# Coarse and fine factor tables of an S4D kernel stored the other way round, with a new order of the work

## The chip, the cores and the metric

The kernel runs on one core of one Trainium2 chip. The metric is the time of one execution on the device in microseconds (us); lower is better. The core's engines work side by side, each through its own list of instructions: TensorE (PE in the profile, with PEld for its weight loads), VectorE (DVE), ScalarE (ACT), GpSimd (POOL) and SyncE (SP), which issues most DMAs here. They wait for each other through semaphores.

## What is computed

The reference is one layer of two blocks on a sequence of 2048 positions with 512 channels, in float32. The first is a diagonal state-space convolution, done with Fourier transforms; the second is a gated MLP:

```python
P = exp((A * dt[:, None])[:, :, None] * pos)         # 512 channels x 128 states x 2048 positions
K = 2.0 * einsum("dn,dnl->dl", C, P).real            # the convolution's kernel
y = irfft(rfft(u, 2L) * rfft(K, 2L))[:L] + u * D_skip
h = x + y(layernorm(x))
z = gelu(layernorm(h) @ w_in)                        # two halves z1, z2
g = w_sp @ layernorm(z2) + b_sp                      # w_sp is 2048 x 2048
out = h + (z1 * g) @ w_out
```

The change touches only the first block, where `P` and `K` are made, and the passage to the second. `A` has a negative real part (the rate of decay) and an imaginary part (the turning).

## The kernel before

**The first block** (`phase_a`) works on the channels in four chunks of 128. For each chunk it makes `K` in eight units of 16 channels (`unit`), and takes `K` and the normed input through transforms that are matrix products: `piece_c` and `piece_d` for `K`, `piece_a` and `piece_b` for the input, the product of the two spectra in `piece_d` (the VectorE multiplication in place in `trio`), and `piece_e` back into `big`. Each kind has eight pieces to a chunk. The spectrum of the input is needed with its two partition halves also swapped; `exchange` makes this copy with two DMAs of 1 MB, `b[:64] <- a[64:]` and `b[64:] <- a[:64]`.

In a unit, sine and cosine come from ScalarE, and the decay from GpSimd. A position is split in two: exp(-rate * position) is a coarse factor times a fine factor. `table` makes all 34 factors for 64 channels (three GpSimd multiplications of rates with the constants `c_lt`, one ScalarE Exp, and one GpSimd multiplication of the last factors with the states' weights). It keeps them in a tile `mt` of [34 factors, 64 channels]: factor by factor, so that two factors of one channel lie 64 numbers apart. A unit then makes three products of 16 channels x 32 positions (8 coarse x 4 fine factors) into `m_bufs`, which lie in the tile `wa`:

```python
ta = mt[:, a0:a0 + 4, d0:d0 + 16].rearrange("p s d -> p d s").unsqueeze(2).to_broadcast([P, 16, 8, 4])
tb = mt[:, b0:b0 + 8, d0:d0 + 16].rearrange("p s d -> p d s").unsqueeze(3).to_broadcast([P, 16, 8, 4])
nc.gpsimd.tensor_tensor(m[:, i, :].rearrange("p (d b a) -> p d b a", d=16, a=4), tb, ta, op=ALU.mult)
```

**The order of the first block** is written out. Every operation is first recorded in a `Plan`. Three tables of characters then say at which place each operation is issued (`RANKS`), on which of two engines it runs where there is a choice (`FORMS`: a copy out of PSUM on ScalarE or VectorE; part of the layernorm's scaling on ScalarE or GpSimd; some small subtractions and products on VectorE or GpSimd) and which PSUM bank it takes (`BANKS`). All of them are issued from `Plan.issue`, which is why nearly every row of this block names line L251.

**The end of the first block.** The last chunk's spectra are multiplied in two parts, channels 0 to 23 and 24 to 31 of each group of 32 (`split`), so that six of the eight pieces back can run before the last units are done. Operations after the last one that touches a generator's buffer (`cut`) are issued by `rest`. Beside them the first weight `w1` of the second block is split into a rounded and a remaining half (`w1h`, `w1l`): four quarters, each a ScalarE copy and a VectorE subtraction, in the buffers `wa` and `wb`. They are issued after the last spectrum product and after the copy out of the piece back numbered 6. The second block starts with `lines` (matmuls into `y`), which read all of `big`.

**The second block** (`phase_b1` to `phase_b3`) is the larger part of the span. Its code and order are left as they are.

## Time and profile before

| | us |
|---|---|
| median of 3 runs | 869.35 (867.56 to 872.04) |
| the profiled execution, its own time | 870.07 |
| span of its instructions | 868.3 |
| first matmul of `lines` (second block) | 321.16 |
| PE busy, share of the span | 808.4, 93% |
| DVE, ACT, POOL busy | 658.1, 467.2, 326.9 |

The profile gives for each engine how long it was busy, in which groups of instructions, and after which wait each one started. "Releaser" is what ended a wait. "issue" stands for time in which the engine waited for nothing that the profile shows. PEclk is the clock that TensorE was granted, 1.00 being the full one. Times in the timeline count from the start of the span. A matmul of float32 numbers stands as two instructions in the timeline (a piece back has 8 products and 16 instructions). DMA queue q1 carries what SyncE issues; q8 carries instructions to the engines, 16 KB in a packet.

### The profile page before, as it was taken

Reading aid. Unit: us, or ns where it says so; the run is one execution under the profiler, and the core shown is the slowest. Engines: PE = TensorE matmul, PEld = TensorE weight load, DVE = VectorE, ACT = ScalarE, POOL = GpSimd, SP = SyncE. Lnnn points to the kernel's source line nnn. Section 1 sums busy time; section 2 is a strip of 40 time slices with the busy share of each in tenths; the row PEclk is TensorE's granted clock in tenths of the full one; section 3 lists DMA queues with packets and bytes.
Section 4 is the critical chain, followed back from the end, with each engine's and each line's share of the span. In section 5 each row is a group of like instructions: output and inputs, shape, how many; then the busy total and the mean of one; then the engine's idle time right before and its main releaser. Section 6 shows DMA issues by size and latency. Waiting matters only on the chain.

```text
span 868.3 us, 17467 instructions
## 1 busy us (share of the span) xinstructions
PE 808.4 (93%) x6813; PEld 694.9 (80%) x6813; DVE 658.1 (76%) x1254; ACT 467.2 (54%) x782; POOL 326.9 (38%) x338
## 2 busy tenths in 40 slices
PE   1379989999898989999999999999999999999998
PEld 0267879889796989888899988888888888887886
DVE  6889999999797539776056778989875985777733
ACT  6679879999897323436223245557434533344211
POOL 6879879999887100000015210123312002223200
PEclk9989999999999979999999999999999999999999
DMA  9212422401307556735216314799979547799832
GB/s 340 76 76 64 100 64 66 108 24 27 84 2 205 205 211 195 182 85 200 92 50 151 80 50 130 178 205 233 239 174 231 187 133 181 158 198 239 207 102 80
DMA packets 63874, 121.81 MB, mean 140 GB/s; under 512 B 6736, under 2 KB 21200, under 8 KB 61488
## 3 DMA queue, kind: packets, MB, share of 16 engines
q1 hardware_dynamic: 52160, 99.33, 37.6%
q0 software_dynamic: 11632, 21.37, 15.1%
q8 instruction: 53, 0.87, 0.4%
q14 instruction: 29, 0.24, 0.1%
HBM read 92.89 MB, written 19.40 MB: 129 GB/s over the span
## 4 chain that ended last, share of the span: by engine, by line
PE 59%; DMA 2%; DVE 1%; issue 0%; ACT 0%; SPq 0%; DVEq 0%; ACTq 0%; POOLq 0%
PE m L1139 28%; PE pz L834 9%; PE pz L934 9%; PE po L1062 7%; PE y L747 4%; PE pl L1062 2%; DMA raws<-in_w_sp_dram 1%; DMA zo<-scr_z 1%; DVE c L1154 0%; DVE c L1092 0%; DVE gz L672 0%; PE lnh_pv L778 0%; DVE wts L672 0%; PE lnh_pm L764 0%; DVE zc_wb L672 0%
## 5 line engine op out<-in xcount | busy, mean ns | idle before, releaser
L1139 PE MATMUL m<-wts,zc_wa 128*128 128x512 f32 x700 | 217.5, 390 | 0.0
L1139 PEld LDWEIGHTS m<-wts,zc_wa 128*128 128x128 f32 x700 | 131.4, 188 | 28.0
L251 POOL TENSOR_TENSOR wa<-mt 128x512 f32<-128x512 f32 x96 | 148.1, 1565 | 12.4 <-PE ps L251 4.6
L1010 POOL DMA_DIRECT2D raws<-in_w_sp_dram x64 | 58.1, 996 | 210.3 <-DMA raws<-in_w_sp_dram 207.7
L1139 PE MATMUL m<-wts,zc_wb 128*128 128x512 f32 x350 | 136.5, 390 | 0.0
L671 ACT CAST wts<-raws 128x512 fp32r<-128x512 f32 x112 | 69.0, 619 | 55.3 <-DMA raws<-in_w_sp_dram 27.2
L672 DVE TENSOR_TENSOR wts<-raws,wts 128x512 fp32r<-128x512 f32 x112 | 76.4, 684 | 16.4 <-ACT wts L671 16.3
L934 PE MATMUL pz<-w,ht 128*128 128x448 f32 x384 | 77.4, 363 | 0.0
L1139 PEld LDWEIGHTS m<-wts,zc_wb 128*128 128x128 f32 x350 | 65.7, 188 | 14.1
L940 POOL TENSOR_SCALAR sm<-sm 128x1 f32<-128x1 f32 x16 | 5.5, 343 | 188.7 <-DVE sm L939 188.7
L934 PEld LDWEIGHTS pz<-w,ht 128*128 128x128 f32 x384 | 72.0, 187 | 5.3
L834 PE MATMUL pz<-ht,w1h 128*128 128x512 f32 x224 | 71.2, 395 | 0.0
L251 ACT ACTIVATE ps<-wb 128x512 f32<-128x512 f32 (+1 forms) x80 | 65.6, 826 | 9.6 <-DVE trio L251 4.1
L251 PE MATMUL ps<-c_inv,trio 128*128 128x128 f32 x512 | 63.4, 282 | 1.3 <-DVE trio L251 1.3
L1062 PE MATMUL po<-w,gz 128*128 128x512 f32 x252 | 62.8, 396 | 1.4 <-DVE gz L672 1.4
L251 PEld LDWEIGHTS ps<-c_inv,trio 128*128 128x128 f32 x512 | 60.6, 196 | 4.3 <-DVE trio L251 1.9
L251 PE MATMUL ps<-big,a 128*128 128x128 f32 (+2 forms) x512 | 63.4, 283 | 0.5 <-ACT big L251 0.2
L251 PEld LDWEIGHTS ps<-big,a 128*128 128x128 f32 x512 | 60.5, 196 | 3.2 <-ACT big L251 0.9
L671 ACT CAST zc_wa<-raws 128x384 fp32r<-128x384 f32 (+1 forms) x70 | 37.1, 533 | 40.9 <-DVE raws L1044 26.1
L1062 PEld LDWEIGHTS po<-w,gz 128*128 128x128 f32 x252 | 47.2, 188 | 13.2 <-DVE gz L672 1.8
L251 ACT COPY big<-ps 128x512 f32<-128x512 f32 x56 | 32.1, 581 | 34.9 <-PE ps L251 34.6
L251 DVE TENSOR_TENSOR trio<-ps,trio 128x1024 f32<-128x1024 f32 (+2 forms) x36 | 38.1, 1104 | 15.8 <-PE ps L251 15.8
(163 smaller groups left out, 1570.3 us busy)
## 6 DMA issues: line engine op xcount, KB each, us to landing
raws<-in_w_sp_dram SPq DMA_DIRECT2D x112, 256.0 KB, 4.1
raws<-in_w_sp_dram POOLq DMA_DIRECT2D x80, 256.0 KB, 5.7
trio<-trio SPq DMA_DIRECT2D x8, 1024.0 KB, 9.5
g<-in_c_g_dram SPq DMA_DIRECT2D x8, 1024.0 KB, 6.3
scr_z<-zo SPq DMA_DIRECT2D x28, 256.0 KB, 2.3
big<-in_u_a_dram SPq DMA_DIRECT2D x8, 512.0 KB, 6.8
xq<-in_u_b_dram SPq DMA_DIRECT2D x4, 1024.0 KB, 6.7
scr_h<-xq SPq DMA_DIRECT2D x16, 256.0 KB, 5.1
```

What stands on the lines that cost most here:

```text
L251: r = getattr(getattr(self.nc, e), method)(*map(self.real, args), **{k: self.real(x) for k, x in kw.items()})
L671: nc.scalar.copy(hi, src)
L672: nc.vector.tensor_sub(lo, src, hi.bitcast(F32))
L747: nc.tensor.matmul(ys[n, g][:, i, :], gt[:, i, r, :], qv[:, r, l0 + i], start=(r == 0), stop=(r == 1))
L834: nc.tensor.matmul(pt, w[:, q, f], ht[n][k][:, q], start=(q == 0 and i == 0), stop=(q == 3 and i == 2))
L934: nc.tensor.matmul(pt[:, :FQ], a[:, q], w2[:, b, q, f], start=(q == 0 and i == 0), stop=(q == 3 and i == 2))
L940: nc.gpsimd.tensor_scalar_add(sm[:, 14:15], sm[:, 13:14], 1e-5)
L1010: nc.gpsimd.dma_start(r, ws[1], accum_op=ALU.add)
L1062: nc.tensor.matmul(pt, gz[fb][x][:, P * a:P * a + P], wo[:, y, fb, w], start=(first and fb == fbs[0] and i == 0), stop=(last and fb == fbs ...
L1139: nc.tensor.matmul(pt, x[:, f], y, start=(k == 0 and i == 0), stop=(k == KT - 1 and i == 2))
```

## The change

- `mt` becomes [64 channels, 34 factors]: the factors of one channel lie next to each other. There are now 4 coarse and 8 fine factors to 32 positions, where there were 8 and 4. The products are written in runs of eight fine factors, and the number of factors stays 34. The multiplications that make the table have the same number of elements (748 + 714 + 714 = 2176, as 768 + 704 + 704 before); the one with the weights has 256 where it had 512.
- `exchange` gets an order between its two DMAs: the second now waits until the first has landed (`two["after"] = one`, "half by half").
- The last chunk's spectra are multiplied in two parts of 16 and 16.
- The quarters of `w1` are split one by one, each right after a copy out of one of the last chunk's last four pieces back.
- `RANKS`, `FORMS` and `BANKS` are new throughout. Three scalings of the layernorm go from GpSimd to ScalarE, three subtractions from GpSimd to VectorE, three copies from ScalarE to VectorE and two small ones too. ScalarE's table loads go from 15 to 18 ahead of the second block.

Three places of the new order, each with the names as the order lists them.

**ScalarE at the end of the first block**, before and after. `big<-ps` is the copy out of a piece back, `w1h<-w1r` the rounding of quarters of `w1`, x4 four of them in a row. Before:

```order
L251 COPY big<-ps_103 128x128x4
L251 COPY big<-ps_101 128x128x4
L251 COPY big<-ps_100 128x128x4
L251 COPY big<-ps_102 128x128x4
L671 CAST w1h<-w1r 128x896 x4
L251 COPY big<-ps_100 128x128x4
```

Now:

```order
L250 COPY big<-ps_101 128x128x4
L250 COPY big<-ps_100 128x128x4
L675 CAST w1h<-w1r 128x896 x2
L250 COPY big<-ps_102 128x128x4
L675 CAST w1h<-w1r 128x896
L250 COPY big<-ps_100 128x128x4
L675 CAST w1h<-w1r 128x896
```

Four roundings stood ahead of the last copy out of a piece back. Now one stands directly ahead of it, and one behind.

**SyncE at the second of the four exchanges**, before and after, with the semaphores that each DMA waits for. `trio<-trio` is half an exchange, `sw` a unit's matmul weights, `wa<-scr_xhat` the normed input of a later piece. Before:

```order
L251 DMA trio<-trio 64x4096 [waits DMAHW7_49,DVE_49,PE_49]
L251 DMA trio<-trio 64x4096 [waits DMAHW0_49]
L251 DMA wa<-scr_xhat 128x256 [waits DMAHW1_49,PE_49]
L251 DMA sw_91<-scr_stk 96x512 [waits DMAHW5_49,DMAHW2_49,PE_49]
L251 DMA wa<-scr_xhat 128x256 [waits DMAHW3_49,PE_49]
```

Now:

```order
L250 DMA trio<-trio 64x4096 [waits DMAHW7_49,DVE_49,PE_49]
L250 DMA trio<-trio 64x4096 [waits DMAHW7_49,DMAHW0_49]
L250 DMA sw_91<-scr_stk 96x512 [waits PE_49]
L250 DMA wa<-scr_xhat 128x256 [waits DMAHW2_49,PE_49]
L250 DMA wa<-scr_xhat 128x256 [waits DMAHW3_49,PE_49]
```

The second half has the first half's semaphore (DMAHW7) among those it waits for, and the loads behind it on SyncE wait with it.

**TensorE behind the last unit**, whose last product is the row `wa,wb`. `ks` is the first transform of `K` (`piece_c`), `big,a` the second (`piece_d`), `c_inv` the way back (`piece_e`), `y` the second block. Before:

```order
L251 MATMUL ps_102<-wa,wb 32x64 x16
L251 MATMUL ps_100<-c_inv,trio 128x128 x8
L251 MATMUL ps_101<-c_inv,trio 128x128 x5
L251 MATMUL ps_103<-wb,ks_81 64x128 x8
L251 MATMUL ps_101<-c_inv,trio 128x128 x3
L251 MATMUL ps_100<-c_inv,trio 128x128 x8
L251 MATMUL ps_102<-big,a_78 128x4x8 x16
L251 MATMUL ps_103<-big,a_78 128x4x8 x16
L251 MATMUL ps_101<-c_inv,trio 128x128 x8
L251 MATMUL ps_102<-c_inv,trio 128x128 x8
L251 MATMUL ps_100<-c_inv,trio 128x128 x8
```

Now, up to the fourth of eight pieces back (four more `c_inv` rows of x8 follow, and then `y`):

```order
L250 MATMUL ps_100<-wa,wb 32x64 x16
L250 MATMUL ps_102<-wb,ks_80 64x128 x8
L250 MATMUL ps_100<-wb,ks_81 64x128 x8
L250 MATMUL ps_101<-c_inv,trio 128x128 x8
L250 MATMUL ps_103<-c_inv,trio 128x128 x8
L250 MATMUL ps_102<-big,a_78 128x4x16 x8
L250 MATMUL ps_100<-big,a_78 128x4x16 x8
L250 MATMUL ps_101<-c_inv,trio 128x128 x8
L250 MATMUL ps_103<-big,a_78 128x4x16 x8
L250 MATMUL ps_102<-big,a_78 128x4x16 x8
L250 MATMUL ps_100<-c_inv,trio 128x128 x8
```

Behind the last product stood 48 products of pieces back; now there are 64, and one more `ks` row. The 32 of `big,a` stay.

The diff, with the tables cut to a line each:

```diff
 RANKS = (
-    "06000407010V090G0M050P0A0J080D0d0Z0g03020B0E0F0H0I0K0L0N0O0T0W0Y0a0c0R0e0f0i0j0l0q0s0v0z0+1011121415181T1I1X221e2326292D"
+    "05000608010709040B0F0A0R0M0V0I0f0Z0j03020C0E0G0H0J0K0L0O0Q0S0U0X0Y0a0N0b0d0m0g0l0o0r0u0z10121316181A1D1Y1O1a1d1h1t221w25"
...
     lt = np.concatenate([
-        28 - 4 * np.arange(8), 1 + np.arange(3), 3 - np.arange(4), 64 * (1 + np.arange(3)),
-        32 + 4 * np.arange(8), 256 * np.arange(8),
+        24 - 8 * np.arange(4), 1 + np.arange(7), 7 - np.arange(8), 64 * (1 + np.arange(7)),
+        32 + 8 * np.arange(4), 512 * np.arange(4),
     ]).astype(f8)
...
     def issue(self, o):
...
+        if "after" in o:
+            info = mybir.DependencyInfo(mybir.DependencyClass.Sync, mybir.DependencyReason.DATA)
+            self.tc.add_manual_dep(r.ins, o["after"]["ins"].name, info, reason="half by half")
+        o["ins"] = r.ins
         return r
...
-    mts = [one(g1, f"mt{h}", [34, 64]) for h in range(2)]
+    mts = [one(g1, f"mt{h}", [64, 34]) for h in range(2)]
...
-        for lo, n in ((0, 12), (12, 11), (23, 11)):
-            nc.gpsimd.tensor_tensor(mt[:, lo:lo + n], rc[:, 64 * h:64 * h + 64].unsqueeze(1).to_broadcast([P, n, 64]),
-                                    c_lt[:, lo:lo + n].unsqueeze(2).to_broadcast([P, n, 64]), op=ALU.mult)
+        for lo, n in ((0, 22), (22, 21), (43, 21)):
+            nc.gpsimd.tensor_tensor(mt[:, lo:lo + n], rc[:, 64 * h + lo:64 * h + lo + n].unsqueeze(2).to_broadcast([P, n, 34]),
+                                    c_lt.unsqueeze(1).to_broadcast([P, n, 34]), op=ALU.mult)
         nc.scalar.activation(mt, mt, AF.Exp)
-        nc.gpsimd.tensor_tensor(mt[:, 26:34, :], mt[:, 26:34, :],
-                                rc[:, P + 64 * h:P + 64 * h + 64].unsqueeze(1).to_broadcast([P, 8, 64]), op=ALU.mult)
+        nc.gpsimd.tensor_tensor(mt[:, :, 30:], mt[:, :, 30:],
+                                rc[:, P + 64 * h:P + 64 * h + 64].unsqueeze(2).to_broadcast([P, 64, 4]), op=ALU.mult)
...
-        for i, (a0, b0) in ((2, (14, 26)), (0, (7, 18)), (1, (11, 0))):
-            ta = mt[:, a0:a0 + 4, d0:d0 + 16].rearrange("p s d -> p d s").unsqueeze(2).to_broadcast([P, 16, 8, 4])
-            tb = mt[:, b0:b0 + 8, d0:d0 + 16].rearrange("p s d -> p d s").unsqueeze(3).to_broadcast([P, 16, 8, 4])
-            nc.gpsimd.tensor_tensor(m[:, i, :].rearrange("p (d b a) -> p d b a", d=16, a=4), tb, ta, op=ALU.mult)
+        for i, (a0, b0) in ((2, (18, 30)), (0, (3, 26)), (1, (11, 0))):
+            ta = mt[:, d0:d0 + 16, a0:a0 + 8].unsqueeze(2).to_broadcast([P, 16, 4, 8])
+            tb = mt[:, d0:d0 + 16, b0:b0 + 4].unsqueeze(3).to_broadcast([P, 16, 4, 8])
+            nc.gpsimd.tensor_tensor(m[:, i, :].rearrange("p (d b a) -> p d b a", d=16, a=8), tb, ta, op=ALU.mult)
...
     def exchange(c):
         a, b, _ = spectra(c)
-        nc.sync.dma_start(b[:64], a[64:])
-        nc.sync.dma_start(b[64:], a[:64])
+        one = nc.sync.dma_start(b[:64], a[64:])
+        two = nc.sync.dma_start(b[64:], a[:64])
+        two["after"] = one
...
         e = evac(o, pt.rearrange("p d r -> p r d"))
-        if s == 6:
-            last[0] = e
-
-    last = [None, None]
+        if c + 1 == NCH and s >= 4:
+            last.append(e)
+
+    last = []
...
-        split = [(0, 32)] if c + 1 < NCH else [(0, 24), (24, 8)]
+        split = [(0, 32)] if c + 1 < NCH else [(0, 16), (16, 16)]
...
-    def rest():
-        done = {}
-        for o in order[cut:]:
-            done[o["rank"]] = nc.issue(o)
-            if o in last and all(x["rank"] in done for x in last):
-                yield [done[x["rank"]] for x in last]
+    def rest(between):
+
+        with tc.manual_schedule(engines={E.PE, E.DVE, E.Activation, E.Pool}):
+            for o in order[cut:]:
+                nc.issue(o)
+                if o in last:
+                    next(between)
...
-    for ev, mul in rest():
-        with tc.issue_after(mul.ins), tc.issue_after(ev.ins):
-            for q in range(4):
-                split(nc, w1h[:, q], w1l[:, q], w1r[:, q])
+    rest(split(nc, w1h[:, q], w1l[:, q], w1r[:, q]) for q in range(4))
```

More of the change, by code (lines that the diff above doesn't have):

```diff
@@ new lines @@
+    "272H2L0y2O0-192N2Q2e2a2V2X2h2n2p2k1c1i1u1x1+280W0T0D0P0k0c0p0v0s1Q1S1T2y1K141U1f2q3C0w1k1B24371V0q1P170t1H1l0x111I151J1F"
+    "1G0+1e0n1N1Z0h0e0i1b1W1M1R1E1C1X1g1j1m1o1s1z20232E26292G2I2J2M2P2R2S2U2W2Y2Z2c2b2r2d3G383H3V2o2f2t3R3d2z3K3T452j3p4G313I"
+    "3J3u3B2i343v2g2l3M4L3O2m2v3f302u3X3P323E3b1q1L2-393U1n3A3S2+3Q2B1v1r2D2s1-363D352F2A1p2w3e2x333h3l3q3t3y3r3+4047494A4B4C"
+    "4D4F4H4J4K4M4N4O4P4Q4Z4n5G5X4j4U5A5Q4l4W5e4w4o5J4c4V4p4Y51564-4t4k525D4T4b4R4d4e5L4S4a5k5o5r67631y3Z2K3F3N3Y3c3g3j3n3m3o"
@@ new lines @@
+    "3z44484I4r4v4x5B5E5I5N5R5S6268435T5g5x6I6M6m6Z6R6j6h6T6e6X5C5h6Y7K7Q7U3a4E413-4X4f5Y5w6H6k6r6o6s6y73777N7D7W7Z7a7g7j7l7q"
+    "7u8K8w74856l8L9DAZAyAgB5AqAzB3AeAkA+B9AiAuAnBCArBF7m7v9uA6AxBID7EVEb5P5s5V5l4+584g4s5K5j4q50595M535Z646C5-6A6q6+7I7P8B8M"
+    "757R8Z8r848G8x9V424h4m4u4z555U3x2T2C544y575d5H5b5i5q8s8v9K3L3w4i5O5a5p5t463i215f5W5c6W5v5+6b6t889J9Y3W3k3s696E6V6K5n6D5z"
+    "6G6O6U6g6c6Q6v7F7t8-9q5F5y616f6n706w666x6p7A76787G7B7H7M7X7c9M9W6-7S7f727n8S7C7J7O7V7d837k6d797E7b7h7s8N8D7p8Q8V8g9p9x7w"
@@ new lines @@
+    "7-868O8W8c8i7L7z898X8U8b8o8h8n8t8y90949F878C8H8+92969A8F8Y8j9895939P9B9O9S9Z9t9wA08k8p8z9L9Q9a9e8u99919b9U9R9n9g9o9-A3A8"
+    "AAAF8q9GAL9+ATAd5m656F6L6z716P6a5u606J6S6i6u6B6N7Y807i7o7r7+8E8J818A7T7x7e8d7y82AfAoASAYAaAhAPAUAVAwAXAbAMARAHANB-C7C5CF"
+    "BdBwB0BECGCNBDBOBkBtBQBXCOCt9C9I9N9k9sA19z9T9d9l9r9v9yA2A7A9AjAsBJDJDUA5ABAGB1B7BLBHAEAlAWBGB8BBBWBPBMBYBeBoDADM9iA4ACAK"
+    "AOApAcAQBKAtA-BUB4BuBZB2BxC1CSCaCeBNBRBVBbBfBlBjBTBhBcBgBpBiBzBrBmCWCZCmDiDoBSCABqBvCTDIBaBnByC2C6C9CCBAC0C4CEC8CBCYCHCM"
@@ new lines @@
+    "CjCqDBDFDRBsB+C3CJCKCpCPCICoCgCQCwCrC-CzCUD3D6D9E9EQCDCfCkD8DDDLDOCVCvD0DGDEDKDXDQDVDeDjDzE4EBCsCyD2DWDbDuDqCcDPDCDfDmDc"
+    "D+DyDwE3EFEMESEYCxDdEpEeEwF88I8R8P8T8f8a8e8l8m9X9h9f979H9EADAIAJ9c9m9jAmAvB6CLCbCnD1D5DHDNDTCuD4ChClCdCiCRCXF7FCE+F9EsEz"
+    "EoF2F1F6EfEmEcEhF5FIG7GaFOFXF+G9FWFlGcGoGMGUFcFkGGGNGmHJDrDxE2E8EaElEgEODlDsEXECEGEuEqEkExF0FDFHGPC+DkDpE1EHETELD-EEE6EA"
+    "EUEJEyEdERFAFEFpHXHgEZEnEtF4FGFMFJEvE-F3FTFNFRFjFZFSFtGCGlGwHDFKFPFVFaFdFgFnEWFFFLFiFeFfFvFoFuFzF-GnG-HFFQFrFYFhH7I3FmFs"
@@ new lines @@
+    "FxG1G3GBGLFbG2FyG4GAG6GTGEGQGVGfHNHSHjFqFwG0GDGHGXGRG8GJGFGIGbGKGjGhGYGpGyH9HCHHG5GOGSGiGrH1G+GWGgGqGuGtGzHIH6H2HQHTHbHh"
+    "HoGZGdGkGvH5HMHVHEGxHAHPH3HKHaHWHZHfHiHlHnHtGeHOHsH+I5IeDSDYDZDaDhDgDnE7DtDvE5E0EIEiEPEDENEKFBFUEjErHLHRHuI0H8HcINITH4HB"
+    "IXIcGsH0IUIZHyI2I4IFIEIII7IAIHIMH-I6I9IWIBIPIbIhIqJ9J5JCIlIzIxJ4JOJXJFJPIgIoJYK5HGHYHeHkHpHvI1I8HUHdIDHqHwIJHzIGILIOIQJo"
+    "JtHrHxIdIjIvJ1I-ICIiHmJ0IsI+JBJ6J3JDJGJSJcJpIRIVIaIfInItIrIKIYISImIpIkJWIwIuJZJsJyK1K9J2J8JAJEJIJTJNJ7JKJHJJJaJMJiJeJRJm"
@@ L71 @@
-    "5545514242534222243453411341005353113230052431155400245210453102445133231552353235442"
+    "345242325433352143423545214452504241024301533511252002324002530153541153500454513444540422555312244155253325542112321132"
+    "550042511524200223104222114331134452011043535413345514544522240544511323002434005541124251143001452201245002523545235425"
+    "43212345422135332045255112430043341135311342200545113524004441124223250353252444523"
 )
@@ L286, in phase_a @@
     sws = [one(g1, f"sw{h}", [4, NS]) for h in range(2)]
-    mts = [one(g1, f"mt{h}", [34, 64]) for h in range(2)]
+    mts = [one(g1, f"mt{h}", [64, 34]) for h in range(2)]
     f_bufs = [one(g1, f"f{i}", [3, W]) for i in range(3)]
     big = Q.tile([P, 4, SLOT], F32, tag="Q", name="big")
-    nc = Plan(tc.nc, [one(ps, f"ps{i}", [2, W] if i < WIDE else [W]) for i in range(8 - WIDE)])
+    nc = Plan(tc, [one(ps, f"ps{i}", [2, W] if i < WIDE else [W]) for i in range(8 - WIDE)])
     def bank(nm, shape):
@@ L593, in piece_d @@
         v = spectra(c)[2].rearrange("p i (d k) -> p i d k", d=32)[:, :, lo:lo + n, 4 * kn * g:4 * kn * g + 4 * kn]
-        last[1] = nc.vector.tensor_mul(v, pt.rearrange("p d k q -> p d (k q)").unsqueeze(1).to_broadcast([P, 2, n, 4 * kn]), v)
+        nc.vector.tensor_mul(v, pt.rearrange("p d k q -> p d (k q)").unsqueeze(1).to_broadcast([P, 2, n, 4 * kn]), v)
     def piece_e(c, s):
```

37 lines of the change are left out of this document (7 added, 30 removed).

## The prediction, as it stands on record

> **What bounds the kernel now.** I read the busy time by stretches first, then the list of waits, then the timeline at the longest waits. The change ends where the second block's first matmul starts, at 321.16 us, so I look at what is ahead of it. Busy time of each engine in stretches of the first block (columns: stretch, its length, busy us and instructions of PE, PEld, DVE, ACT, POOL, then granted clock, DMA share, GB/s):
>
> ```profile
> 60.00:140.00 80.00, 74.59 (x1329) 65.28 (x1318) 76.08 (x109) 69.44 (x101) 67.59 (x61) 1.00 0.36 93
> 140.00:200.00 60.00, 58.70 (x1086) 51.12 (x1085) 57.98 (x77) 56.81 (x72) 58.33 (x49) 1.00 0.24 57
> 200.00:260.00 60.00, 57.73 (x901) 52.41 (x903) 54.41 (x69) 54.62 (x69) 53.04 (x44) 0.97 0.18 40
> 60.00:320.00 260.00, 245.24 (x4107) 219.15 (x4095) 222.21 (x294) 207.61 (x278) 198.98 (x171) 0.97 0.35 96
> ```
>
> From 140 to 200 us all four engines are above 94%. TensorE is the fullest over the whole stretch: it idles 260.00 - 245.24 = 14.8 us. Its work isn't changed (as many matmuls as before), so what the change can bring is mostly in these 14.8 us, in clock that is lost around them, and in the start before 60 us. What TensorE waited for, and what VectorE waited for from GpSimd (us in total, times, longest):
>
> ```profile
> PE ps L251 <- issue: 6.8, 3, 3.5
> PE y L747 <- ACT big L251: 2.7, 1, 2.7
> PE ps L251 <- DVE f L251: 2.0, 3, 0.9
> PE ps L251 <- DVE wb L251: 1.7, 2, 1.4
> ...
> DVE f L251 <- POOL wa L251: 0.2, 1, 0.2
> ```
>
> Of the 14.8 us, 6.8 are three waits with no releaser and 2.7 is the last wait ahead of `y`. The rest is 14.8 - 6.8 - 2.7 = 5.3 us in small pieces. For GpSimd's products VectorE waited 0.2 us in all: GpSimd is nearly full, but late for nobody.
>
> The three waits, with SyncE's exchanges beside them (start, length, row):
>
> ```profile
> 113.81 1.42 PE L251 MATMUL ps<-wb,ks 128*64 128x128 f32 x21 [1.36 <-issue]
> 225.66 0.44 PE L251 MATMUL ps<-wa,wb 128*32 128x64 f32 x7 [1.92 <-issue]
> 277.29 0.91 PE L251 MATMUL ps<-wa,wb 128*32 128x64 f32 x25 [3.54 <-issue]
> ...
> 98.96 1.18 SPq L251 DMA_DIRECT2D trio<-trio  x2
> 148.65 1.12 SPq L251 DMA_DIRECT2D trio<-trio  x2
> 213.63 0.47 SPq L251 DMA_DIRECT2D trio<-trio  x1
> 214.78 51.15 SPq L251 DMA_DIRECT2D trio<-trio  x3
> ```
>
> TensorE stops in the middle of a row of equal matmuls, 12 to 15 us after an exchange was begun (the fourth is the last of the three at 214.78, whose end is 265.93). That looks like a sequencer that has run out of instructions. The DMA queues while an exchange ran, at the first and the third (packets, MB, share of 16 engines), and in the 1.5 us after the third:
>
> ```profile
> q1 hardware_dynamic: 359, 2.13, 96.1%
> ...
> q1 hardware_dynamic: 224, 1.77, 75.4%
> ...
> q8 instruction: 1, 0.02, 5.6%
> ```
>
> From 100.9 to 111.1 us and from 212 to 222.5 us the only queue listed is q1; the next packet of instructions comes at once behind, and TensorE goes on after it. The second exchange had no such wait, so the reading is likely, not certain. After two of the three stops the clock was halved for 3 us:
>
> ```profile
> 225.70:228.70 3.00, 3.00 (x47) 2.01 (x48) 0.37 (x1) 2.52 (x3) 1.67 (x3) 0.50 0.02 5
> 277.30:280.30 3.00, 3.00 (x45) 2.83 (x46) 1.10 (x3) 0.00 (x0) 1.56 (x2) 0.50 1.00 391
> ```
>
> **The change part by part.**
>
> *The end of the block.* ScalarE's four roundings stand ahead of the last copy for which `y` waits:
>
> ```profile
> 317.16 3.46 ACT L671 CAST w1h<-w1r 128x896 fp32r<-128x896 f32 x4
> 320.52 0.58 ACT L251 COPY big<-ps 128x512 f32<-128x512 f32 x1
> 321.16 10.82 PE L747 MATMUL y<-big,g 128*128 128x128 f32 x80 [2.73 <-ACT big L251]
> ```
>
> In the new order one rounding (3.46 / 4 = 0.87 us) and one copy (0.58) lie between the last two pieces back: 1.45 us. A piece back is 16 instructions, and 32 take 3.73 us (row below), so a piece takes 1.87 us and ScalarE is ready in time. What is left is the copy and 0.06 us, 0.64 us of the 2.73: **-2.1 us**. If the copy still waits for one rounding, -1.2; no more than -2.7 can go.
>
> *The exchange in halves.* With one half under way, a packet of instructions has 1 MB in front of it and not 2. The pair lands in 9.5 us (below), so about half of that, 4.7 us, is saved on the instructions, more than any of the three stops. I take 1.36 + 1.92 and half of 3.54, since three loads of 1 MB still follow the last exchange directly: **-5.0 us**, bounds 0 and -6.8. The clock: 3 us at 0.50 lose 1.5 us after each of two stops, 3.0 in all, of which I take half: **-1.5**, bounds 0 and -3.0. What it costs is a later second half; rows of 1 MB transfers, and of TensorE's work that covers them:
>
> ```profile
> trio<-trio SPq DMA_DIRECT2D x8, 1024.0 KB, 9.5
> xq<-in_u_b_dram SPq DMA_DIRECT2D x4, 1024.0 KB, 6.7
> ...
> 255.20 0.71 PE L251 MATMUL ps<-c_k,sw 96*128 96x512 f32 x2
> 255.75 3.73 PE L251 MATMUL ps<-c_inv,trio 128*128 128x128 f32 x32
> 259.88 0.65 PE L251 MATMUL ps<-f 128*32 128x64 f32 x32
> 289.91 1.09 PE L251 MATMUL ps<-wb,ks 128*64 128x128 f32 x16
> ```
>
> Two halves one after the other take 9.5 us if the pair filled the engines, and 2 x 6.7 = 13.4 if each goes as a lone load of 1 MB does. The new order puts the least work between exchange and first spectrum product in the last chunk: six `ks` rows (6.5 us), three phase products (2.1) and eight rows of generator products (8 x 0.65 = 5.2), 13.8 us of TensorE. Cover of 13.8 against 9.5 to 13.4 us: **0**, and what it costs without the cover is a rival below. SyncE's queue behind the waiting half holds `sw` and inputs of later pieces, which have at least as long.
>
> *GpSimd.* Its groups of instructions (busy us, mean ns of one):
>
> ```profile
> L251 POOL TENSOR_TENSOR wa<-mt 128x512 f32<-128x512 f32 x96 | 148.1, 1565 | 12.4 <-PE ps L251 4.6 <-DVE f L251 2.3 <-DVE wb L251 2.2
> L251 POOL TENSOR_TENSOR mt<-rcs,wb 128x704 f32<-128x704 f32 x16 | 21.9, 1372 | 7.1 <-DVE rcs L251 7.1
> L251 POOL TENSOR_TENSOR wb<-wb,wa 128x512 f32<-128x512 f32 x16 | 20.7, 1292 | 6.8 <-ACT wb L251 6.3 <-DVE f L251 0.4
> L251 POOL TENSOR_TENSOR mt<-mt,rcs 128x512 f32<-128x512 f32 x8 | 10.3, 1293 | 0.0
> L251 POOL TENSOR_TENSOR ks<-ks,wb 128x4 f32<-128x4 f32 x32 | 6.6, 216 | 21.4 <-ACT ks L251 15.3 <-DVE ks L251 6.1
> ```
>
> A product of two full streams of 512 costs 1292 ns; one with a repeated operand costs (1372 - 216) / 704 = 1.64 ns an element, which gives 216 + 512 x 1.64 = 1056. The old product costs more than either, and it alone reads factors that lie apart. The new one reads neighbours and repeats the other operand: between 1056 and 1292, I take the middle, 1.17 us. That takes 96 x 0.39 = 38 us off GpSimd (26 to 49), and the eight weight products of 256 elements (636 to 754 ns for 1293) another 5. For the end of the block this is **0** by itself, because nobody waited for GpSimd; it makes room in which the new order can lose less than the 5.3 us of small waits: bounds 0 and -5.3.
>
> [...]
>
> *What the new order adds.* Three more table loads on ScalarE:
>
> ```profile
> L251 ACT ACT_TABLE_LOAD x15 | 19.2, 1283 | 1.0 <-PEq L1245 0.7
> ```
>
> 3 x 1.28 = 3.8 us, and ScalarE idles 260.00 - 207.61 = 52 us in the stretch: **0**, at most +3.8. Behind the last generator product stand 16 more products of pieces back, 32 instructions (3.7 us), and one more `ks` row (1.09). It is work that stood ahead of it before, so it costs **0** if the last unit is earlier by that much, which the stops and the earlier place of the last unit's products in VectorE's list (ahead of seven of the eight last spectrum products, where all eight stood in front) allow; +4.8 if it isn't.
>
> **Sum** against the profiled execution, 870.07 us: -2.1 - 5.0 - 1.5 = -8.6, 861.5. The median is 0.7 lower, so 869.35 - 8.6 = 860.8; I say **861 us**.
>
> **The rivals.**
>
> *The stops stay.* If the packets of instructions don't wait for the exchange (the second exchange speaks for this, since none of TensorE's waits without a releaser follows it), halving it changes nothing. Left is -2.1: 867.2. [...] The stretch 100.9 to 111.1 us, with nothing but q1 in it, speaks against that.
>
> *GpSimd was the brake.* If the small waits exist because a full GpSimd left the order no choice, all 5.3 us go as well: 869.35 - 8.6 - 5.3 = 855.5. Against it stands the 0.2 us.
>
> *The product is no faster.* Then the table's layout doesn't do what it says: in the last four units 12 products run 0.39 us longer than the order counted on, 4.7 us ahead of the end: 865.5. The two rows with neighbouring reads, both under 1300 ns, speak against.
>
> *The halves in series come too late: slower.* If a half alone takes as long as the pair, 9.5 us, the second lands 19 us after the exchange began, 5 us past the 13.8 us of cover in the last chunk. A second chunk has about 15 us of work there (six input pieces, four `ks` rows, generator rows), and 4 us are lost. The stops stay too, since the engines are as long engaged: 869.35 - 2.1 + 5 + 4 = 876.3. It decides from a half of 7 us on (2 x 7 is past 13.8). The lone 1 MB load of 6.7 us is just under it; the 96.1% for the pair says that half the bytes take about half the time.
>
> **How the numbers follow.** Forecast 0.48 (own range 856 to 865); stops stay 0.24; GpSimd the brake 0.10; product no faster 0.08; halves too late 0.10. To hold eight of ten, the range goes from 854 (the brake, with some more) to 870 (the stops stay, with small waits of the new order); the too late halves lie above it. About 0.5%, 4.3 us, is what can be told from no change here, so faster means under 865.0. Faster: 0.48 x 0.92 + 0.24 x 0.12 + 0.10 = 0.57. Slower, over 873.7: 0.10 and 0.03 for an order that loses elsewhere, 0.13. The rest, 0.30, is the same.
>
> **What would show it.** In the changed kernel's profile: the wait of `y` for ScalarE falls from 2.7 to about 0.6 us; the waits with no releaser on TensorE fall from 6.8 to under 2, and the clock stays above 0.50 behind the exchanges; `y` starts near 312 us. The products `wa<-mt` stand at 1.06 to 1.29 us each, GpSimd's busy time at 326.9 - 43 = 284 us. Wrong would be: waits of VectorE's `trio` for a DMA `trio` (halves too late), waits of VectorE's `f` for `wa` (products late), or stops that stay at 6.8. From `y` on nothing changes, about 549 us; a difference there would be none of these.

## The result, and the profile after

| | before | after |
|---|---|---|
| median, us | 870.31 (867.56 to 872.04) | 846.41 (844.69 to 848.59) |
| span of the profiled execution, us | 868.3 | 842.9 |
| first matmul of `y`, us | 321.16 | 297.40 |

The change makes the kernel faster by 23.9 us: ratio 0.973, interval 0.969 to 0.977. The forecast was 8.6 us in the right direction, and 846.4 lies below its range. In the two profiled executions 23.8 us are gained ahead of `y` and 1.6 behind it (545.5 us for 547.1).

First, TensorE's time up to `y` in two parts. Busy time by stretches, the kernel before; the first row is the whole way to `y`, the others are the five stretches in which the clock stood at 0.50, four of them ahead of `y` and one that begins with it (columns: stretch, length, busy us and instructions of PE, PEld, DVE, ACT, POOL, then granted clock, DMA share, GB/s):

```profile
0.00:321.16 321.16, 266.58 (x4249) 236.35 (x4249) 271.27 (x463) 248.49 (x362) 243.43 (x226) 0.97 0.36 107
51.60:58.40 6.80, 5.93 (x56) 5.93 (x58) 5.46 (x10) 2.92 (x7) 3.43 (x6) 0.50 0.01 2
225.70:229.10 3.40, 3.40 (x50) 2.41 (x50) 0.42 (x1) 2.92 (x3) 1.94 (x5) 0.50 0.02 5
276.90:280.30 3.40, 3.01 (x45) 2.83 (x46) 1.10 (x3) 0.00 (x0) 1.56 (x2) 0.50 0.98 381
307.60:314.40 6.80, 6.80 (x34) 6.80 (x34) 1.23 (x1) 0.00 (x0) 0.00 (x0) 0.50 0.25 72
321.30:324.70 3.40, 3.40 (x17) 3.40 (x18) 0.99 (x1) 0.00 (x0) 0.00 (x0) 0.50 1.01 426
```

The same view of the changed kernel:

```profile
0.00:297.40 297.40, 253.57 (x4248) 228.45 (x4248) 268.25 (x469) 251.14 (x363) 194.99 (x220) 1.00 0.39 113
60.00:297.40 237.40, 229.12 (x3986) 208.13 (x3984) 214.94 (x286) 203.00 (x266) 152.78 (x165) 1.00 0.36 98
```

As many matmuls (4249 and 4248) take 266.58 - 253.57 = 13.0 us less busy time, and TensorE idles 54.6 - 43.8 = 10.8 us less. The four stretches at half clock ahead of `y` add up to 20.4 us, so up to 10.2 of the 13.0 us can be clock; the changed kernel has none ahead of `y` in its profiled execution. The other 2.8 us I can't assign. The fifth stretch, 3.4 us, lies behind `y`, and half of it, 1.7 us, is about what is gained there.

The same rows show how much earlier the work was done. At 60 us the kernel before had 4107 instructions of TensorE left (row 60.00:320.00 of the prediction), the changed kernel 3986. It is 121 instructions ahead there; at 229.12 / 3986 = 57 ns each that is a head start of 7.0 us (an estimate).

TensorE's waits in the changed kernel from 60 us to `y` (us in total, times, longest):

```profile
PE ps L250 <- DVE trio L250: 2.1, 3, 0.9
PE ps L250 <- DVE wa L250: 1.8, 5, 0.7
PE ps L250 <- DVE big L250: 1.6, 2, 1.1
PE ps L250 <- DVE f L250: 1.0, 2, 0.7
PE ps L250 <- ACT big L250: 0.8, 1, 0.8
PE y L748 <- ACT big L250: 0.7, 1, 0.7
```

The three waits with no releaser (6.8 us) are gone. No wait for a DMA is among them, and VectorE's `trio` has none for an exchange either, so no half of an exchange comes late. The end of the block, timeline of ScalarE and TensorE:

```profile
294.92 0.59 ACT L250 COPY big<-ps 128x512 f32<-128x512 f32 x1 [3.10 <-PE ps L250]
295.40 0.94 ACT L675 CAST w1h<-w1r 128x896 fp32r<-128x896 f32 x1
296.76 0.58 ACT L250 COPY big<-ps 128x512 f32<-128x512 f32 x1 [0.42 <-PE ps L250]
297.40 1.83 PE L748 MATMUL y<-big,g 128*128 128x128 f32 x14 [0.73 <-ACT big L250]
```

One rounding stands ahead of the last copy and doesn't delay it; `y` waits 0.73 us for the copy, where it waited 2.73. GpSimd's groups and the exchange, from the page (busy us, mean ns of one; for the DMA KB each and us from issue to landing):

```profile
L250 POOL TENSOR_TENSOR wa<-mt 128x512 f32<-128x512 f32 x96 | 107.3, 1131 | 35.2 <-PE ps L250 15.6 <-DVE wb L250 13.9 <-DVE trio L250 1.6
L250 POOL TENSOR_TENSOR mt<-mt,rcs 128x256 f32<-128x256 f32 x8 | 5.2, 655 | 1.7 <-ACT mt L250 1.7
...
trio<-trio SPq DMA_DIRECT2D x8, 1024.0 KB, 6.9
```

A product takes 1131 ns for 1565, the weight product 655 for 1293. A lone half lands in 6.9 us where the pair took 9.5.

### The profile page after: what moved, and what is told of

It is laid out like the page before. It is cut to its first block, busy times and chain, and to the rows that moved or that the text cites. A ratio compares the mean times of both kernels' runs of the same rounds, so it can differ in the third digit from the quotient of the medians.

```text
span 842.9 us, 17463 instructions
## 1 busy us (share of the span) xinstructions
PE 794.1 (94%) x6813; PEld 685.6 (81%) x6813; DVE 654.2 (78%) x1260; ACT 469.1 (56%) x783; POOL 278.5 (33%) x332
## 4 chain that ended last, share of the span: by engine, by line
PE 67%; DVE 14%; DMA 7%; issue 6%; ACT 5%; POOL 1%; SPq 1%; DVEq 0%; ACTq 0%; POOLq 0%
PE ps L250 20%; PE m L1140 18%; PE pz L835 9%; PE pz L935 9%; DMA raws<-in_w_sp_dram 6%; PE po L1063 5%; DVE trio L250 4%; PE y L748 3%; PE pl L1063 2%; ACT wb L250 2%; DVE wts L676 1%; ACT big L250 1%; ACT ps L250 1%; DVE wb L250 1%; DVE f L250 1%
## 5 line engine op out<-in xcount | busy, mean ns | idle before, releaser
L250 POOL TENSOR_TENSOR wa<-mt 128x512 f32<-128x512 f32 x96 | 107.3, 1131 | 35.2 <-PE ps L250 15.6
L250 PE MATMUL ps<-big,a 128*128 128x128 f32 (+1 forms) x512 | 62.4, 278 | 0.9 <-DVE trio L250 0.8
L250 PE MATMUL ps<-c_inv,trio 128*128 128x128 f32 x512 | 60.6, 277 | 1.3 <-DVE trio L250 1.3
L250 PEld LDWEIGHTS ps<-c_inv,trio 128*128 128x128 f32 x512 | 58.8, 192 | 3.2 <-DVE trio L250 1.9
L835 PEld LDWEIGHTS pz<-ht,w1h 128*128 128x128 f32 x224 | 42.1, 188 | 9.2
L1045 DVE TENSOR_TENSOR raws<-z 128x384 f32<-128x384 f32 (+1 forms) x80 | 46.1, 584 | 0.3
```

Of the source, the lines that this page charges most:

```text
L250: r = getattr(getattr(self.nc, e), method)(*map(self.real, args), **{k: self.real(x) for k, x in kw.items()})
L835: nc.tensor.matmul(pt, w[:, q, f], ht[n][k][:, q], start=(q == 0 and i == 0), stop=(q == 3 and i == 2))
L1045: nc.vector.tensor_tensor(zs[:, :w], x, y, op=op)
```

## The experiments

All times are medians; "before" is 870 to 873.5 us in each series, and ratios are to it. Because "before" moves by some 3 us from series to series, kernels of different series are better compared by their ratios than by their times.

**1. The halves alone, in the old order.** As in the change, for whichever half comes second in the order:

```diff
-        nc.sync.dma_start(b[:64], a[64:])
-        nc.sync.dma_start(b[64:], a[:64])
+        one = nc.sync.dma_start(b[:64], a[64:])
+        two = nc.sync.dma_start(b[64:], a[:64])
+        one["mate"], two["mate"] = two, one     # the one issued second waits for the first
```

> The kernel before, with one thing of the change: whichever half of an exchange is issued second waits until the first has landed. The theory of the forecast (instructions queue behind 2 MB of exchange): the three stops of TensorE with no releaser (6.8 us) are gone, and with them the two half-clock stretches behind them; 860 to 863 us against 870.3. The rival (the stops have another cause, the new order moved the time): stops as before or elsewhere, 868 to 872 us. Halves too late: waits of TensorE or VectorE for a trio DMA, over 873.

Measured 863.29 us, 0.992 (0.989 to 0.994): 7.3 us by the ratio. Waits of TensorE:

```profile
PE y L752 <- ACT big L251: 2.7, 1, 2.7
PE ps L251 <- issue: 2.7, 2, 1.6
PE ps L251 <- DMA wa<-scr_xhat: 1.6, 1, 1.6
```

The stops (`issue`) fall from 6.8 to 2.7 us, and the two stretches of half clock behind them are gone: up to `y` TensorE is busy 262.77 us for 266.58, 3.8 less, at a mean clock of 0.98 for 0.97. The last row is new: TensorE once waits for a load of input, which the forecast had put at no cost. The forecast's 5.0 + 1.5 for this part was right in mechanism. That its sum fits is in part luck: the stops gave 4.1, the two stretches of 3.4 us at half clock gave more than 1.5, and the late load took some of it back.

**2. The change without the halves.**

```diff
-        two["after"] = one
```

> The changed kernel without the wait between the halves of an exchange; all else, the order too, as changed. If instructions queue behind 2 MB: at least two of the four exchanges bring a stop with no releaser and a half-clock stretch, 851 to 856 us against 846.4. If the new order has its need for instructions elsewhere, or the wait was never the point: within 1 us of 846.4.

Measured 855.06 us, 0.982 (0.976 to 0.987), 8.7 us above the changed kernel by the medians and 7.4 by the ratios. Waits and the first two stops:

```profile
PE ps L250 <- issue: 5.9, 4, 2.3
```

```profile
110.27 0.65 PE L250 MATMUL ps<-wb,ks 128*64 128x128 f32 x6 [0.34 <-issue]
158.12 2.18 PE L250 MATMUL ps<-wb,ks 128*64 128x128 f32 x35 [1.03 <-issue]
```

Now there are four stops for the four exchanges, with one behind the second (the other two take 2.31 and 2.25 us). The second had none in the kernel before, which spoke for the rival "the stops stay"; here it has one too. The halves are worth 7 to 9 us in either order.

**3. The new tables alone, in the old order.** The four hunks on `lt`, `mts`, `table` and the products, nothing else.

> The kernel before in its old order, with the new table layout and the products in runs of eight alone. If nobody waited for GpSimd: products of about 1.13 us for 1.57, GpSimd's busy time some 45 us lower, time within 1.5 us of 870.3. If GpSimd was the brake in the old order too: 860 to 866.

Measured 873.35 us, 1.003 (1.000 to 1.006).

```profile
L251 POOL TENSOR_TENSOR wa<-mt 128x512 f32<-128x512 f32 x96 | 107.1, 1132 | 35.7 <-PE ps L251 19.0 <-DVE wb L251 8.8 <-DVE f L251 5.2
```

With 41 us less work on GpSimd nothing is gained: it only waits more (35.7 us ahead of these products, 12.4 before). "0 by itself" was right.

**4. The change with the old tables.** The same four hunks taken back.

> The changed kernel in its new order, with the old table layout and products (1.57 us each). If GpSimd's speed carries nothing: within 1.5 us of 846.4. If the new order was built on the faster products: VectorE waits for wa, and 10 to 25 us of the gain are gone (856 to 871). My number is 856: GpSimd has 153 us of work in 237 us of span now, and 45 more would leave it 83 per cent busy, not enough to keep its place in every unit.

Measured 849.18 us, 0.975 (0.970 to 0.980); a product again takes 1561 ns. That is 2.8 us above the changed kernel by the medians and 2.0 by the ratios, and the intervals overlap. So what the tables bring in the new order, if anything, is at most a few us, and the new order hardly needs the faster GpSimd. The expectation was far off here: with GpSimd as slow as before, 21 us are gained.

**5. Parts of 24 and 8 in the new order.**

```diff
-        split = [(0, 32)] if c + 1 < NCH else [(0, 16), (16, 16)]
+        split = [(0, 32)] if c + 1 < NCH else [(0, 24), (24, 8)]
```

with places for the eight, two, six and two pieces. The first part is here computed before two of the pieces that it reads have been copied, so the values aren't the reference's; the work is.

> The changed kernel with the last chunk's spectra again in parts of 24 and 8, at the places of the new order (the second group of four of the first part shares its PSUM banks with the first, which may cost 1 to 2 us). Two kernels of the old order lose half of their clock for 6.8 us while the part of 8 runs (matmuls of 32 columns). If these narrow matmuls are the cause: a half-clock stretch at the end of the first block, y 3 to 5 us later, 849 to 852 us against 846.4. If the old order's waits were the cause: clock 1.00 throughout, 846 to 848.

Measured 859.27 us, 0.986 (0.981 to 0.992), with stretches at half clock at 256.9 to 263.9 (0.51), 277.4 to 281.0 (0.53) and 297.9 to 304.9 us (0.51). It is 13 us slower than the changed kernel, but it has a stop of 1.97 us too, and a first part that now has twice as many multiplications on VectorE; it shows that the tail of the new order depends on its parts. The last of the three stretches is the one that the theory named: it begins inside the row of matmuls of 32 columns, 291.82 to 299.98 us (see behind number 11). The other two were not expected.

**6. The roundings ahead of the last copy again, in the new order.**

```diff
-                if o in last:
-                    next(between)
+                if o in last and o is [x for x in order[cut:] if x in last][-2]:
+                    for _ in between:
+                        pass
```

> The changed kernel with all four roundings of w1 ahead of the last copy again, as in the kernel before. By the forecast's first term: the wait of y for ScalarE goes from 0.73 to about 2.7 us, 848.4 us. If the end is bound elsewhere: no change.

Measured 848.19 us, 0.974 (0.968 to 0.979), and `y`'s wait is back at 2.73 us: the mechanism of the term of -2.1 is shown. Its size in time is not: the kernel is 1.8 us above the changed one by the medians and 0.4 by the ratios, and its profiled execution also has a stop of 1.97 us that the changed kernel's lacks.

```profile
301.30 2.94 PE L749 MATMUL y<-big,g 128*128 128x128 f32 x24 [2.73 <-ACT big L250]
```

**7. Tables and halves, in the old order.** Edits 1 and 3 together.

> The kernel before in its old order with two things of the change, the new table and the exchange in halves. If the faster GpSimd brings nothing even where no stop hides it: as with the halves alone, 862 to 865 us. If GpSimd was the brake behind the stops: 855 to 860.

Measured 863.57 us, 0.993 (0.989 to 0.996): as the halves alone. By now some 17 of the 24 us belong to what the forecast priced at -2.1: the new order, with the parts of 16 and 16 and the places of the roundings.

**8. The start's clock, in the old order.** The last matmul of the second and third input piece is repeated eight times (it writes the same numbers again), to fill the gaps there:

```diff
...
+    for o in first[1:3]:
+        o["calls"] = o["calls"] + 8 * [o["calls"][-1]]
```

> The kernel before, with the last matmul of the second and of the third input piece repeated eight times into the same place (same values), so that TensorE has work in the two gaps of 1.4 us at 48 to 52 us. In the kernel before these gaps are followed by 6.8 us at half clock. If the gaps are the cause: clock 1.00 from 52 us on, the first pieces done 2 to 3 us earlier; the time 866 to 869 against 870.3 as far as the later units can use it. If they are not: the same half-clock stretch, time as before or 1 us more.

Measured 872.72 us, 1.002 (0.999 to 1.005). Busy time and clock in two stretches:

```profile
51.60:58.40 6.80, 6.80 (x102) 6.63 (x101) 5.66 (x11) 3.77 (x11) 3.35 (x6) 1.00 0.01 2
112.10:118.90 6.80, 5.77 (x58) 4.95 (x60) 2.34 (x4) 4.72 (x4) 4.36 (x4) 0.50 0.01 3
```

The clock at the start is full, but it brings little: the row `c_k,sw` that started at 108.61 us starts at 107.84, 0.8 us earlier. That is lost by 119 us: the stops grow to 8.8 us in two (3.15 and 5.63), and from 112.1 us, inside the first of them, the clock is at half for 6.8 us (second row). Why they grow was not tried.

**9 to 11. The old order with its losses taken away one by one**, all with the halves: parts of 16 and 16 (two of the pieces back moved behind the second part); the filled start; and both, with the roundings behind the last copy.

```diff
-        if s == 6:
+        if s == 7:
...
-        split = [(0, 32)] if c + 1 < NCH else [(0, 24), (24, 8)]
+        split = [(0, 32)] if c + 1 < NCH else [(0, 16), (16, 16)]
...
+    for o in first[1:3]:
+        o["calls"] = o["calls"] + 8 * [o["calls"][-1]]
```

The first of these three edits is in number 11 only, the second in 9 and 11, the third in 10 and 11. In 9 and 11 the first of the second part's four transforms is issued one place ahead of the copy of its last input piece, so the values aren't the reference's; the work is.

> The kernel before with the exchange in halves, and the last chunk's spectra in parts of 16 and 16 in place of 24 and 8, the rest of the order as before (two of the eight pieces back move behind the second part). Up to the first matmul of y, TensorE was busy 266.58 us before and 253.57 us in the changed kernel, for 4249 and 4248 matmuls: 13.0 of the 23.8 us are busy time, and most of that is clock. Theory (narrow matmuls halve the clock): the 64 instructions of 32 columns run in a stretch of 6.8 us at 0.50, and y's first 3.4 us follow at 0.50 too. With 64 columns both stretches go: 3.4 + 1.7 us less than the halves alone, about 858 us, y about 5 us earlier, and no 0.50 between 290 us and y. Rival (the order, not the width): the stretch at 0.50 stays or moves, and the two pieces back behind the second part cost up to 2 us: 863 to 866 us.

> The kernel before with the exchange in halves, and the last matmul of the second and of the third input piece repeated eight times, which kept the clock full at 52 to 58 us in the kernel before, but whose 3 us were given back at longer stops. Theory (the start's clock counts once the stops are gone): 3 us less than the halves alone, about 860 us, and TensorE ahead by 3 us from 62 us to y. Rival (another engine sets the pace from 60 us on, so an early TensorE waits): 863 us, as with the halves alone.

> The kernel before with four things and its own order of the units: exchange in halves, start filled, parts of 16 and 16, and the four roundings of w1 behind the last copy out of a piece back. Theory (the gain of the changed kernel is mostly clock and stops, which add up): 863.5 - 3 - 5 - 2 = 853.5 us, no stretch at 0.50 of more than 3.4 us, and 7 us left to the changed kernel's 846.5 for what else its order does. Rival (only the new order as a whole has it, since VectorE, ScalarE and GpSimd set the pace in the old one): 860 us or more.

Measured: 868.29 (0.996, 0.993 to 0.999), 864.39 (0.993, 0.990 to 0.996) and 861.52 us (0.992, 0.988 to 0.995). All three miss their first theory. Number 9's profiled execution has TensorE at half clock for 13.6 us, almost all of it where the kernel before had it full (from 280.3 us on), with matmuls of 64 columns:

```profile
279.40:293.00 13.60, 13.60 (x71) 13.15 (x71) 6.24 (x7) 0.58 (x1) 0.00 (x0) 0.50 0.52 215
```

Waits of 1.73 and 0.38 us stand just ahead of it. So narrow matmuls aren't needed for a stretch at half clock. One of its ten executions took 859.15 us at a mean clock of 1.000, the others 867 to 870 at 0.985 to 0.988: with the clock full this kernel is 8 to 11 us shorter, and the clock falls differently from one execution to the next. Number 11's profiled execution keeps it full from 51 us to `y`:

```profile
51.60:312.92 261.32, 246.45 (x4210) 220.32 (x4209) 228.34 (x303) 210.04 (x286) 203.76 (x178) 1.00 0.34 95
```

and that execution still took 860.18 us, 14 more than the changed kernel. My second theory, that the gain is mostly clock and stops, falls with it: with the clock full and 2.2 us of stops left, the old order is 14 us slower (2.2 of them the repeated matmuls, by an estimate: 32 instructions at 68 ns, as in a row of 16 in 1.09 us).

One pattern shows only when the profiled executions of the kernels here, the later numbers too, are put side by side. With parts of 24 and 8 the clock falls to half inside the row of 64 instructions of 32 columns in the kernel before (6.8 us, from 307.6), in number 5 (7.0 us at 0.51, from 297.9) and in number 10 (10.3 us, from 298.9). In numbers 1, 7, 16 and 17 that row and the 48 instructions `c_inv,trio` behind it take 15.9 us together, as in the kernel before (17.6 in number 10), which makes the loss there the same 3.4 us (an estimate). The row in the kernel before:

```profile
302.51 9.06 PE L251 MATMUL ps<-big,a 128*128 128x32 f32 x64
```

With 16 and 16 the last part shows no half clock in the nine that were read there. The clock is 1.00 in stretches that reach to `y`, or to 1.2 us ahead of it, in the changed kernel and in numbers 4, 11 and 15. In numbers 6 and 12 to 14, 32 instructions of 64 columns take 3.68 us in the last part, as in number 4, and in number 9, 48 take 5.47, as in number 11. So narrow matmuls aren't needed, but half clock came in each of the seven rows of them: 6.8 us of it in the kernel before, 3.4 us lost, which the parts of 16 and 16 can save at this place. Number 9 shows that the clock can fall elsewhere instead (279.4 to 293.0 us).

**12 to 15. The old order in front, the new one behind.** The changed kernel, with the first 284, 387, 777 or 1185 of its 1380 recorded operations in the order of before, on the engines and banks of before, and the rest in its own order. The kernels hold the finished tables; this is the rule by which they were made (not a line of the kernels):

```python
order = before[:n] + [o for o in after if o not in before[:n]]
```

> The changed kernel, with the first 284 of its 1380 recorded operations in the order (and on the engines and PSUM banks) of the kernel before, and the others in its own order. That is the preparation up to the first input pieces: TensorE reached them at 46.3 us before and at 45.3 us in the changed kernel. Theory (each stretch of the new order saves its own share, which stays saved): 1 us lost, 847.5 us. Rival (the gain is made in the last chunk, by what stands behind the last unit, and an early delay is caught up): 846.5 us. Rival (the start's preparation carries it all the way): 852 us.

> The same with the first 387 operations in the order of before: up to TensorE's 149th matmul, which started at 66.0 us with the exchange in halves and the old order, and at 62.0 us for the same count in the changed kernel; the input pieces come in three bits as before, with TensorE at 0.50 from 52 to 56 us. Theory: 4 us lost, 850.5 us, y at 301.5. Rival (caught up): 847 us.

> The same with the first 777 operations: 827 of 2160 matmuls, reached at 147.9 us in the old order with halves and at 141.4 us in the changed kernel. Theory: 6.5 us lost, 853 us, y at 304. Rival (caught up): 847 us; rival (all that is gained, is gained ahead of here): 858 us or more.

> The same with the first 1185 operations: 1652 of 2160 matmuls, reached at 243 us in the old order with halves; only the last chunk's end is the changed kernel's. By the work done (weighted by the mean time of each matmul) the old order stands 10 to 12 us behind there. Theory: 11 us lost, 857 us, and the clock stays at 1.00 from there to y. Rival (the end alone makes most of the gain): 849 us.

| old order up to about | us | ratio (interval) | adds, us |
|---|---|---|---|
| nothing (changed kernel) | 846.41 | 0.973 (0.969 to 0.977) | |
| 46 us | 856.86 | 0.983 (0.979 to 0.987) | 8.4 |
| 65 us | 857.98 | 0.984 (0.980 to 0.988) | 0.9 |
| 148 us | 857.18 | 0.984 (0.979 to 0.989) | 0.3 |
| 243 us | 859.96 | 0.986 (0.981 to 0.992) | 2.1 |
| all (number 7) | 863.57 | 0.993 (0.989 to 0.996) | 5.3 |

The last column is the step between two unrounded ratios times 870; steps of 1 to 2 us lie within the intervals. Each stretch was expected to lose its own share, 1 us of it in the preparation. Most of it goes in one step, the preparation: the first 46 us, in which TensorE has hardly anything to do (busy 10.1 us of them before, 11.0 in the changed kernel). The rival that named it said 852; it came out worse.

Busy time of the stretches 20 to 46 and 46 to 58 us, the kernel before, the changed one, and the changed one with the old preparation:

```profile
20.00:46.00 26.00, 8.42 (x31) 6.36 (x33) 22.84 (x81) 18.21 (x48) 23.14 (x27) 1.00 0.29 87
46.00:58.00 12.00, 9.23 (x96) 8.75 (x94) 9.70 (x19) 8.49 (x18) 8.63 (x13) 0.73 0.01 1
```

```profile
20.00:46.00 26.00, 8.94 (x39) 6.63 (x40) 24.91 (x87) 23.44 (x54) 20.85 (x28) 1.00 0.26 77
46.00:58.00 12.00, 11.98 (x212) 10.84 (x208) 11.41 (x23) 11.69 (x24) 9.81 (x14) 1.00 0.13 49
```

```profile
20.00:46.00 26.00, 8.31 (x29) 6.26 (x31) 22.80 (x81) 17.12 (x46) 18.28 (x26) 1.00 0.26 73
46.00:58.00 12.00, 7.62 (x77) 6.60 (x74) 8.03 (x15) 10.71 (x23) 4.42 (x7) 0.86 0.00 1
```

In the preparation VectorE works 24.9 of 26 us in the new order and 22.8 in the old one, ScalarE 23.4 and 18.2 (17.1). From 46 to 58 us TensorE then runs 212 instructions at full clock, against 96 and 77. Which work was moved shows in VectorE's timeline; before:

```profile
47.56 0.96 DVE L251 RECIPROCAL ps<-trio 128x128 f32<-128x128 f32 x1
48.55 0.30 DVE L251 TENSOR_TENSOR ps<-ps,trio 128x128 f32<-128x128 f32 x1
```

the changed kernel:

```profile
36.42 0.95 DVE L250 RECIPROCAL ps<-trio 128x128 f32<-128x128 f32 x1
37.40 0.30 DVE L250 TENSOR_TENSOR ps<-ps,trio 128x128 f32<-128x128 f32 x1
```

and TensorE's first input pieces, before:

```profile
45.20 3.41 PE L251 MATMUL ps<-wb,big 128*64 128x128 f32 x32 [6.42 <-DVE big L251]
50.03 1.09 PE L251 MATMUL ps<-wb,big 128*64 128x128 f32 x16 [1.42 <-DVE wb L251]
52.47 5.82 PE L251 MATMUL ps<-wb,big 128*64 128x128 f32 x52 [1.35 <-DVE big L251]
```

and in the changed kernel with the old preparation:

```profile
52.25 4.63 PE L250 MATMUL ps<-wb,big 128*64 128x128 f32 x48 [3.26 <-DVE big L250]
...
263.79 0.57 PE L250 MATMUL ps<-f 128*32 128x64 f32 x20 [1.97 <-issue]
```

The chain of small VectorE operations that ends in the reciprocal ran at 46 to 49 us in the old order, between the operations that TensorE's input pieces wait for; in the new order it runs eleven microseconds earlier, where VectorE is busier than it was (24.9 for 22.8 us). In number 12 the wait for this chain can be followed from engine to engine:

```profile
48.48 0.30 DVE L250 TENSOR_TENSOR ps<-ps,trio 128x128 f32<-128x128 f32 x1
48.81 0.26 ACT L250 ACTIVATE ps<-ps 128x128 f32<-128x128 f32 x1 [1.24 <-DVE ps L250]
49.09 1.28 ACT L250 ACT_TABLE_LOAD   x1
51.27 0.46 ACT L250 ACTIVATE ps<-big,wb 128x256 f32<-128x256 f32 x1
51.77 0.43 DVE L250 SCALAR_TENSOR_TENSOR big<-ps,big 128x256 f32<-128x256 f32 x1 [2.65 <-ACT ps L250]
```

ScalarE waits for the end of VectorE's chain, loads a table, comes to what VectorE waits for, and VectorE's result ends TensorE's wait of 3.26 us at 52.25. In the changed kernel the same ScalarE operation, `ps<-big,wb`, ran at 42.21 us. Afterwards the delay stays. The row `c_k,sw` behind the first input pieces starts at 58.10 us in number 12 and at 51.40 in the changed kernel, 6.7 us apart; a row of 80 matmul instructions `c_inv,trio` starts at 239.80 and 232.01, 7.8 apart. `y` starts at 308.14 us, 10.7 after the changed kernel's: the rest comes at the stop of 1.97 us at 264 us, with 3.4 us of half clock behind it (264.2 to 267.6, 0.51).

**16 and 17. The new preparation ahead of the old order**, the opposite joint: number 7, with the first 356 or 383 operations in the changed kernel's order.

> The other way round: the kernel before with the new tables and the exchange in halves, with the first 356 recorded operations in the changed kernel's order, and the others in that of before. In the changed kernel that is the preparation and TensorE's first 85 matmuls, which were reached at 55.0 us there and at 58.9 to 60.1 us in the old order. Tables and halves alone in the old order gave 0.9925 of before, 863.6 us. Theory (half of the unforecast gain is in the preparation, which brings the input pieces in one row and the clock to full from 50 us on, and it stays): 863.6 - 5 = 858.5 us. Rival (the old order behind it can't use an early start, as it could not use the filled one): 863.5 us.

> The same with the first 383 operations: 133 matmuls, reached at 59.5 us in the changed kernel and at 63.5 to 63.9 us in the old order. Theory: 858.5 us as well, since only the preparation matters; rival 863.5 us; more than 2 us below the kernel with 356 operations would put the gain into the first units instead.

Measured 858.43 us (0.985, 0.980 to 0.989) and 858.70 us (0.985, 0.982 to 0.989), as the theory said: 5 us by the medians, 6 to 7 by the ratios. Number 16 from 46 to 58 us:

```profile
46.00:58.00 12.00, 11.69 (x216) 10.66 (x214) 10.31 (x21) 11.31 (x23) 9.02 (x12) 1.00 0.19 71
```

So it is the preparation, and not the joint: it pays in front of either order. And it stays: a row `c_k,sw` that starts at 108.78 us in number 7 starts at 103.30 in number 16, another at 261.32 and 256.45, so 5.5 us are left at 4.9. The filled start of number 10 had the same full clock there, but from 46 to 58 us it ran only 146 instructions, 32 of them repeats that nobody needs, where number 16 ran 216. Its stretch of half clock ahead of `y` (10.3 us, below) was also longer than number 1's: the row of 64 instructions and the 48 behind it took 17.6 us for 15.9, and 1.6 us more is about 3.3 us more at half clock (an estimate).

## Why the prediction was right or wrong

- **End of the block, -2.1:** right as a wait: 0.73 us for the 0.64 forecast, and 2.73 again when undone. In the time, number 6 can't tell it from nothing (0.4 us by the ratios).
- **Exchange in halves, -5.0, and the clock behind the stops, -1.5:** together right for this part by the ratios (7.3 us in the old order, 7.4 in the new one, for 6.5), in part by errors that cancel (number 1). The changed kernel's profiled execution has no stop left, but other kernels with halves still have one or two (0.86 to 1.97 us in numbers 1, 4, 6 and 12). "Halves too late" fell: a half takes 6.9 us, just under the 7 from which the forecast let it decide, and VectorE's `trio` waits 0.3 us for one in number 1 and not at all in the changed kernel.
- **"The stops stay":** fell with numbers 1 and 2. In number 1 halving alone brought the stops from 6.8 to 2.7 us, and in number 2, with both halves let go together, TensorE stopped four times for four exchanges, 5.9 us in all.
- **GpSimd's product, 1.17 us and 0 by itself:** right; 1.13 us, and nothing in the old order. In the new order 2.0 to 2.8 us, within the noise and inside the bounds of 0 and -5.3. (The 5.3 us of small waits are really 6.4: the stretch that was read ends at 320 us, and `y`'s wait at 321.16.) "GpSimd was the brake" fell: with slow products the new order still gives 21 us.
- **What the order adds, 0:** no cost was seen from ScalarE's table loads or the work behind the last unit. The last stretch from 243 us gained 3.6 us by the medians and 5.3 by the ratios. `y`'s wait (2.0) and the half clock on the narrow matmuls (3.4) would make that up, but the profiled executions of numbers 15 and 7 are only 1.0 us apart, so it isn't shown. The forecast had no term for the parts of 16 and 16.
- **The step that failed** is the first one. It says that the change can bring time in the 14.8 idle microseconds behind 60 us, "in clock that is lost around them, and in the start before 60 us", and then the sum has no term for the start: it was put at nothing without a reason. The preparation is worth 5 to 8 us (numbers 12, 16 and 17; 7.0 by the instructions left at 60 us). The second miss is the clock, which I priced only behind two stops (3.0 us) where the five stretches come to 11.9, 1.7 of them behind `y`, where the forecast saw no change. The row for 46 to 58 us was to be had: it shows both, 9.23 busy microseconds of 12 and a clock of 0.73.
- **The rule behind both misses:** a full engine. I read "TensorE idles only 14.8 of 260 us" as a small prize. It also means that there is little idle time in which a delay ahead of that stretch could be caught up, and number 12 shows it: 6.7 us late at 58 us, 7.8 at 240. A filled start is not the same: in number 8 it brought the work forward by 0.8 us, which the next stop took.

What stays open: the steps of numbers 12 to 15 sum up to the gain because each is the difference of two neighbours; between 46 and 243 us they are as small as their intervals, so where the 9 to 11 us beyond halves and preparation come from is known only in part. Which of the operations of the preparation counts (the three scalings on ScalarE, the chain with the reciprocal, the table loads between) wasn't tried apart. Why the clock stays full up to `y` in the changed kernel's profiled execution, and is below full in nine of ten executions of number 9, was not settled.

## What to carry to other kernels

Where one engine is full for most of a stretch, look first at what stands ahead of it: work brought forward there can come out at the end almost whole (5 to 8 us here), while a full clock there, with the work itself no earlier, brought 0.8 us and lost them at the next stop (number 8). Add up every stretch at half clock, not only those behind a wait that you mean to remove (11.9 us lost here, where the forecast saw 3.0). When a new order is the change, price each stretch on its own; the way to find out afterwards is to put the old order back for a first part of the work, and the new one behind it.
